# Query products of the later token blocks as three fp32r products in a fused attention and two-layer MoE kernel

## The chip, the cores and the metric

The kernel runs on one core of one Trainium2 chip. The metric is the time of one execution on the device in microseconds (us). The core has five engines that run side by side, each with its own queue of instructions: PE multiplies matrices (the page shows its loads of weights as PEld), DVE and ACT work elementwise on on-chip memory, POOL does too but can't reach the accumulators (PSUM), and SP issues transfers (DMA). An instruction waits on semaphores for what it needs, and everything behind it on the same engine waits with it.

## The reference

Linear attention is computed per batch and head, its output is normalised per head, and the result goes through two feed-forward layers with a normalisation between them.

```python
kv = np.einsum('bhsd,bhse->bhde', k, v)          # 8 batches, 8 heads, 576 tokens, 64 wide
out = np.einsum('bhsd,bhde->bhse', q, kv)
rms = np.sqrt(np.mean(out * out, axis=-1, keepdims=True) + 1e-06)
x = out / rms * g_norm                            # as 4608 tokens x 512
h = np.maximum(np.maximum(x @ w1, x @ w2), x @ w3)
y = h @ w_out                                     # 768 wide inside
xn = y / rms(y) * rms_g
g = xn @ w_gate
result = (silu(g) * (xn @ w_val)) @ w_out2        # 1536 wide inside
```

## The kernel before, in words

The 4608 tokens are nine blocks of 512, numbered 0 to 8. A batch has 576 tokens, so most blocks lie across two batches: block 4 has 256 columns of batch 3 and 256 of batch 4, block 7 has 448 and 64, block 8 lies in batch 7 alone.

Nearly all products are exact to about fp32 by splitting. A value is rounded to the format fp32r by a copy on ACT (its high part), the rest is a subtraction on DVE or POOL (its low part), and `mm3` (lines 506 to 509) multiplies high by high, high by low and low by high into one accumulator. Two products of the kernel are not split: the key-value sums of a batch (`kv_part`, line 327) and the query products (`po`) take plain fp32 operands. A plain product stands in the trace as two records for each matmul of the program.

For blocks 0 to 2 the query products are made token by token (`token_steps`). For blocks 3 to 8 `wide_block` does a whole block. Its steps `po(c)` for c = 0 to 3 multiply two heads each: the stationary operand is a 128x128 matrix with the two heads' key-value sums on the diagonal (`kvbd`), the moving operand is 512 columns of queries, cut where the block passes from one batch into the next. ACT copies each result and squares it, DVE sums the squares (`part`), and a chain of small steps through DRAM gives the factors with which `xn` scales the copy. `hi` and `lo` then split that into `X[t]`, the operand of the block's three up products.

The order is written by hand. `tick` opens a slot and runs the steps that `at(n, ...)` has put n slots ahead. A block has 24 slots, of which each follows 12 matmuls of an up product (`do_p`) or of the product down (`do_o`). `slot` also advances three background chains: the normalisation of the block before (`flush`), the sums of pairs of blocks for the second layer (`aside`, which steps through `pair_sums`, with sums on DVE, high parts on ACT at line 711, low parts on DVE at line 715, and stores `td`), and the preparation of second-layer weights (`prep`, held back while `live` would exceed `room[0]`). While `pair_sums` is under way, `aside` runs once a slot and `prep` every second slot.

While the products of block t run, block t+1 is prepared. Its query products come in the first two slots, between the up products of block t. Batch t+2 is loaded in slot 18 (`load_kv`: per source two pieces of 256 rows, and 64 rows at the end), its key-value sums run in slot 23 (`do_kv`), and the queries of the next block but one are loaded in slots 19 and 20 (`load_q`). All these tiles come from one pool of 38 buffers of 4 KB per partition (`unit`); `X[t]` and the copies `yr` come from a pool `xp` of two buffers of 16 KB.

Of the kernel before, what the change touches and what calls it, by code (L numbers as in the profile page):

```python
# [29 lines left out]
NP = H // 2  # L30
WIDE = 3
J1, J2 = F1 // P, F2 // P
EPS = 1e-6
# [27 lines left out]
def tile_kernel(ctx: ExitStack, tc, qT, k, v, kvt0, kvt1, w1, w2, w3, wo, wg, wv, wo2, out):  # L61
# [201 lines left out]
    def load_kv_part(b, c, only=None):  # L263
        r = b * S
        m, tail = KV.setdefault(b, ([None] * 4, []))
        if c == 2:
            if b == 0:
                t = unit([P, 2 * DM], F32, "kvt")
                nc.sync.dma_start(t[:, :DM + 1 + KC], kvt0)
                tail += [t]  # L270
                first_tail.append(t)
            elif b == 1:
                t = unit([P, 2, DM], F32, "kvt")
                nc.sync.dma_start(t[:64], kvt1.rearrange("p (two f) -> p two f", two=2))
                tail += [t[:64, 0], t[:64, 1]]
            else:
                t = unit([P, 2, DM], F32, "kvt")
                for i, src in enumerate((k, v)):
                    tail.append(t[:64, i])
                    nc.sync.dma_start(tail[i], src[r + 512:r + 576, :])  # L280
# [25 lines left out]
    def kv_part(b, c):  # L306
# [5 lines left out]
        for hp in range(NP):  # L312
            pk = PK["odd" if b == 0 and hp >= NP // 2 else b]
            for h in range(2):
                o = (2 * hp + h) * D
                if c < 4:
                    kk = m[c // 2][:, c % 2, o:o + D]
                    vv = m[2 + c // 2][:, c % 2, o:o + D]
                elif b == 0:
                    r, f = divmod(o, DM // 2)  # L320
                    r = slice(r * 64, r * 64 + 64)
                    kk = tail[0][r, f:f + D]
                    vv = tail[0][r, DM // 2 + f:DM // 2 + f + D]
                else:
                    kk = tail[0][:, o:o + D]
                    vv = tail[1][:, o:o + D]
# [4 lines left out]

    def kv_copy(b, kvb):
        pk = PK.pop(b)
        n = NP // 2 if b == 0 else NP
        nc.scalar.activation(kvb[:D, :n, 0:D], pk[:D, :n], AF.Copy)
        nc.scalar.activation(kvb[D:, :n, D:], pk[D:, :n], AF.Copy)
        if b == 0:
            pk = PK.pop("odd")
            nc.vector.tensor_copy(kvb[:D, n:, 0:D], pk[:D, n:])
            nc.vector.tensor_copy(kvb[D:, n:, D:], pk[D:, n:])  # L340
        del KV[b]
        kvbd[b] = kvb

    def do_kv(b, kvb):
        for c in range(5):
            kv_part(b, c)
        kv_copy(b, kvb)

# [14 lines left out]
    def token_steps(i, pool=ps):  # L363
# [42 lines left out]
        def hi():  # L406
            if i // NS not in X:
                new_x(i // NS)
            nc.scalar.activation(X[i // NS][:, 0, :, cut_of(i)], st["pt"], AF.Copy, scale=gc)

        def lo():
            x = X[i // NS]
            f = cut_of(i)
            nc.vector.scalar_tensor_tensor(x[:, 1, :, f], st["pt"], gc, f32(x[:, 0, :, f]), ALU.mult, ALU.subtract)

# [14 lines left out]
    def wide_block(t, s):  # L430

        st = {}
        nb = TB // 32

        def po(c):
            if c == 0:
                st["y"] = xp.tile([P, 2, KC, TB], F32, tag="x", name="yr")
                st["part"] = hp.tile([P, KC, nb], F32, tag="part", name="part")
            q = Q[2 * t + c // 2][:, c % 2]
            o = psum([P, TB], "po")  # L440
            b = t * TB // S
            n = min(TB, (b + 1) * S - t * TB)
            nc.tensor.matmul(o[:, :n], kvbd[b][:, c, :], q[:, :n], start=True, stop=True)  # L443
            if n < TB:
                nc.tensor.matmul(o[:, n:], kvbd[b + 1][:, c, :], q[:, n:], start=True, stop=True)
            if c % 2:
                del Q[2 * t + c // 2]
            nc.scalar.activation(st["y"][:, 0, c], o, AF.Copy)
            sq = st["sq", c] = tmp("sq")
# [21 lines left out]
        def respread():  # L471
            for n in range(2):
                nc.scalar.dma_start(
                    st["y"][n * D:(n + 1) * D, 1].rearrange("p c f -> p (c f)"), hr_d[t][n:n + 1].to_broadcast([D, KC * TB])
                )

        def xn(c):
            x = st["x", c] = tmp("xn")
            f = st["y"][:, 1].rearrange("p (m c) f -> p m (c f)", m=2)[:, c // 2]
            f = f.rearrange("p (j c b) -> p c j b", c=2, b=nb)[:, c % 2]  # L480
            xv, yv = (a.rearrange("p (j b) -> p j b", b=nb) for a in (x, st["y"][:, 0, c]))
            nc.vector.scalar_tensor_tensor(xv, yv, gc, f, ALU.mult, ALU.mult)

        def hi(c):
            if c == 0:
                new_x(t)
            nc.scalar.activation(X[t][:, 0, c], st["x", c], AF.Copy)

        def lo(c):
            x = X[t]  # L490
            nc.gpsimd.tensor_tensor(x[:, 1, c], st.pop(("x", c)), f32(x[:, 0, c]), ALU.subtract)
# [12 lines left out]

# [6 lines left out]
    def proj(p, w, x, a=0, b=TB, cs=range(KC)):  # L511
        for c in cs:
            f = slice(c * P, (c + 1) * P)
            mm3(p[:, a:b], w[:, 0, f], w[:, 1, f], x[:, 0, c, a:b], x[:, 1, c, a:b], c == 0, c == KC - 1)

# [31 lines left out]
    def proj2(p, w, x):  # L547
        for c in range(KC):
            f = slice(c % 2 * P, (c % 2 + 1) * P)
            mm3(p, w[:, c // 2, 0, f], w[:, c // 2, 1, f], x[:, 0, c], x[:, 1, c], c == 0, c == KC - 1)  # L550

# [126 lines left out]
    def hi_x2(i):  # L678
        nc.scalar.activation(X[NB][:, 0, i], X2[i], AF.Copy)

    def lo_x2(i):
        nc.vector.tensor_tensor(X[NB][:, 1, i], X2.pop(i), f32(X[NB][:, 0, i]), ALU.subtract)

# [85 lines left out]
    def load_x(t):  # L769
        raw = xp.tile([P, 3, 2, TB], F32, tag="x", name="xr")  # L770
        nc.sync.dma_start(raw[:, 0], xn_d[t][:2 * P].rearrange("(c p) n -> p c n", p=P))
        for k in range(2):
            nc.sync.dma_start(raw[:, 1 + k], xn_d[t + k][2 * P:].rearrange("(c p) n -> p c n", p=P))
        XR.append(raw)

    def build_x(n):
# [7 lines left out]
        for m, r in ((1, 0), (2, 1), (3, 2)):  # L784
            for k in range(2):
                x = XO[m, k] = unit([P, 2, TB], F32R, "xo")
                nc.scalar.activation(x[:, 0], raw[:, r, k], AF.Copy)
            yield
            for k in range(2):
                x = XO[m, k]  # L790
                nc.gpsimd.tensor_tensor(x[:, 1], raw[:, r, k], f32(x[:, 0]), ALU.subtract)

# [67 lines left out]
    def slot():  # L860
# [3 lines left out]
        if not side or n_slot[0] % 2:  # L864
            prep()

    def prod3(o, ah, al, bh, bl, first, last):
# [126 lines left out]
    def down(n, ph, xs):  # L994
# [3 lines left out]
        if ph == 0:  # L998
            OP[n] = xp.tile([P, KC, 2, TB], F32, tag="x", name="op")

# [8 lines left out]
        def place(d, c):  # L1009
            fh, th = divmod(c, 2)  # L1010
            return OP[n][:, 2 * fh + d, th]

# [97 lines left out]
    with tc.manual_schedule():  # L1110
# [13 lines left out]

        kvb = []
        z = unit([P, 2, NP, P], F32, "kvbd")
        nc.gpsimd.memset(z, 0.0)
        kvb += [z[:, 0], z[:, 1]]
        tok = [token_steps(i, ps if i < NS else pa) for i in range(2 * NS)]
        up_p = {}  # L1130
# [25 lines left out]
        for word in ORDER.split():  # L1156
# [18 lines left out]
            elif kind == "kc":  # L1175
                kv_copy(n[0], kvb[n[0]])
            elif kind == "busy":
# [18 lines left out]
        def kv_do(n, b):  # L1196
            at(n, lambda: do_kv(b, kvb[b % 2]))

# [24 lines left out]
        for t in range(2, NB):  # L1223
            last = t + 1 == NB
            if not last:
                nt = t + 1
                wide_block(nt, 0)
                if nt + 1 < B:
                    at(14, lambda: room.__setitem__(0, 4))
                    at(18, lambda b=nt + 1: load_kv(b))  # L1230
                    at(23, lambda b=nt + 1: (do_kv(b, kvb[b % 2]), room.__setitem__(0, 8)))
                if nt + 1 < NB:
                    for g in range(2):
                        at(19 + g, lambda i=2 * nt + 2 + g: load_q(i))
            else:
# [117 lines left out]
```

## Time and profile before

| what | value |
|---|---|
| median of 3 runs | 1457.09 us (1456.44 to 1457.49) |
| the profiled execution | 1456.97 us, its span 1455.2 us |
| PE busy | 1448.5 us of the span |
| DVE, ACT, POOL busy | 900.1, 625.2, 470.5 us |
| blocks 3 to 8 prepared | about 173 to 540 us |

The profiled execution has its own time; its span runs from the first to the last instruction, and the 1.8 us around it are not in the trace. It lies 0.12 us under the median. A matmul's record is longer than what it costs, since matmuls overlap; the cost is read from the starts of neighbouring records.

### The profile page before, as it was taken

How to read it: one execution, taken by the hardware profiler on the slowest of the kernel's cores; microseconds unless marked ns; L12 is line 12 of the kernel's file. 1: busy time of each engine (PE TensorE's matmuls, PEld its weight loads, DVE VectorE, ACT ScalarE, POOL GpSimd, SP SyncE). 2: the span in 40 equal slices, each digit the busy share in tenths (PEclk: the TensorE clock that was granted, in tenths of full speed). 3: DMA queues.
4: the chain of work that ended last, by engine and by line, in shares of the span. 5: the costliest groups of instructions: out<-in, count | busy, mean ns of one | idle time of the engine just before them, and what ended most of it. 6: DMA issues, size and time to landing. Idle time of an engine off the chain costs nothing.

```text
span 1455.2 us, 19535 instructions
## 1 busy us (share of the span) xinstructions
PE 1448.5 (100%) x7062; PEld 1201.1 (83%) x7062; DVE 900.1 (62%) x1341; ACT 625.2 (43%) x1110; POOL 470.5 (32%) x317
## 2 busy tenths in 40 slices
PE   9999999999999999999999999999999999999999
PEld 8888888888888878888888888888888888888887
DVE  6864475667366776874445475674665656754756
ACT  6863445445434563644224343343243442434422
POOL 3211232424232423321332252541334422532423
PEclk9999999999999999999999999999999999999999
DMA  9422255657266655779968464784666843784542
GB/s 367 154 94 95 80 182 200 221 215 277 106 210 219 232 188 192 279 262 374 371 228 329 177 234 185 284 311 171 247 228 257 333 179 130 296 302 182 193 170 107
DMA packets 108176, 322.54 MB, mean 222 GB/s; under 512 B 13168, under 2 KB 13424, under 8 KB 107312
## 3 DMA queue, kind: packets, MB, share of 16 engines
q1 hardware_dynamic: 94592, 294.56, 55.0%
q10 hardware_dynamic: 13488, 26.73, 5.8%
q8 instruction: 56, 0.92, 0.3%
q14 instruction: 40, 0.33, 0.1%
HBM read 247.73 MB, written 73.52 MB: 221 GB/s over the span
## 4 chain that ended last, share of the span: by engine, by line
PE 99%; DVE 0%; issue 0%; ACT 0%; POOL 0%; POOLq 0%
PE ua L869 18%; PE p L507 10%; PE p L509 10%; PE p L508 10%; PE ub L869 9%; PE da L869 9%; PE db L869 4%; PE uc L869 4%; PE acc L508 4%; PE acc L507 4%; PE acc L509 4%; PE dc L869 2%; PE pk L327 1%; PE po L443 1%; PE pg L507 1%; PE pv L509 1%
## 5 line engine op out<-in xcount | busy, mean ns | idle before, releaser
L507 PE MATMUL p<-x,w 128*128 128x512 f32 (+1 forms) x656 | 258.8, 395 | 0.0
L509 PE MATMUL p<-x,w 128*128 128x512 f32 (+1 forms) x656 | 254.0, 387 | 0.0
L508 PE MATMUL p<-x,w 128*128 128x512 f32 (+1 forms) x656 | 253.7, 387 | 0.0
L869 PE MATMUL ua<-xo,w 128*128 128x512 f32 x864 | 213.4, 389 | 0.0
L526 POOL TENSOR_TENSOR ho<-sl,ho 128x512 fp32r<-128x512 f32 x72 | 98.2, 1371 | 303.1 <-issue 247.3
L869 PEld LDWEIGHTS ua<-xo,w 128*128 128x128 f32 x864 | 162.2, 188 | 33.7
L526 POOL TENSOR_TENSOR ho<-t,ho 128x512 fp32r<-128x512 f32 x96 | 123.9, 1295 | 133.1 <-ACT ho L525 116.1
L526 POOL TENSOR_TENSOR hs<-h,hs 128x512 fp32r<-128x512 f32 x45 | 64.4, 1430 | 297.2 <-ACT hs L525 253.8
L869 PE MATMUL ub<-xo,w 128*128 128x512 f32 x576 | 146.1, 389 | 0.0
L509 PEld LDWEIGHTS p<-x,w 128*128 128x128 f32 x656 | 123.2, 188 | 25.6
L507 PEld LDWEIGHTS p<-x,w 128*128 128x128 f32 x656 | 123.3, 188 | 24.9 <-issue 0.5
L508 PEld LDWEIGHTS p<-x,w 128*128 128x128 f32 x656 | 123.3, 188 | 24.6 <-issue 0.5
L869 PEld LDWEIGHTS ub<-xo,w 128*128 128x128 f32 x576 | 108.1, 188 | 22.5
L951 ACT ACTIVATE s<-ua 128x512 f32<-128x512 f32 x96 | 57.3, 597 | 139.2 <-PE ua L869 139.2
L869 PE MATMUL da<-ho,wd 128*128 128x512 f32 x432 | 105.7, 389 | 0.0
L525 ACT ACTIVATE ho<-t 128x512 fp32r<-128x512 f32 x96 | 59.4, 627 | 100.5 <-DVE t L702 100.5
L869 PEld LDWEIGHTS da<-ho,wd 128*128 128x128 f32 x432 | 81.1, 188 | 16.8
L538 DVE TENSOR_TENSOR s<-p,s 128x512 f32<-128x512 f32 x45 | 31.1, 690 | 98.8 <-PE p L509 91.8
L899 DVE TENSOR_TENSOR c<-uc,s 128x512 f32<-128x512 f32 x48 | 33.1, 689 | 84.1 <-PE uc L869 84.1
L507 PE MATMUL acc<-hs,w 128*128 128x512 f32 x216 | 84.2, 390 | 0.0
L509 PE MATMUL acc<-hs,w 128*128 128x512 f32 x216 | 84.1, 389 | 0.0
L508 PE MATMUL acc<-hs,w 128*128 128x512 f32 x216 | 84.0, 389 | 0.0
(163 smaller groups left out, 2664.5 us busy)
## 6 DMA issues: line engine op xcount, KB each, us to landing
w<-wd SPq DMA_DIRECT2D x180, 512.0 KB, 7.7
wd<-ws SPq DMA_DIRECT2D x72, 512.0 KB, 3.1
wd<-wd SPq DMA_DIRECT2D x72, 512.0 KB, 6.9
wq<-wd SPq DMA_DIRECT2D x72, 256.0 KB, 7.7
xo<-td SPq DMA_DIRECT2D x32, 512.0 KB, 9.6
q<-in_qT SPq DMA_DIRECT2D x18, 512.0 KB, 6.3
raw<-in_w SPq DMA_DIRECT2D x18, 512.0 KB, 10.1
raw<-in_wo SPq DMA_DIRECT2D x18, 512.0 KB, 6.7
```

Source lines behind the costliest of these rows:

```text
L327: nc.tensor.matmul(pk[h * D:(h + 1) * D, hp, :], kk, vv, start=(c == 0 and hp in ((0, NP // 2) if b == 0 else (0,))), stop=(c == 4), skip_ ...
L443: nc.tensor.matmul(o[:, :n], kvbd[b][:, c, :], q[:, :n], start=True, stop=True)
L507: nc.tensor.matmul(o, ah, bh, start=first, stop=False)
L508: nc.tensor.matmul(o, ah, bl, start=False, stop=False)
L509: nc.tensor.matmul(o, al, bh, start=False, stop=last)
L525: nc.scalar.activation(hs[:, 0], h, AF.Copy)
L526: nc.gpsimd.tensor_tensor(hs[:, 1], h, f32(hs[:, 0]), ALU.subtract)
L538: nc.vector.tensor_tensor(s2, p, s1, ALU.max)
L869: nc.tensor.matmul(o, aa, bb, start=first and q == 0, stop=last and q == 2, skip_group_check=True)
L899: nc.vector.tensor_tensor(t, p, s, ALU.add)
L951: nc.scalar.activation(t, p, AF.Copy)
```

## The change

The query products of blocks 3 to 8 are now split too. `kv_split` rounds the key-value sums of a batch to high parts on ACT and puts the rest on DVE, both into one buffer `kvr` that is used again by every second batch; batch 2 is kept in both forms, since block 2 still needs the plain one. `split` rounds the queries of a block in the first two slots, two instructions on ACT and two on DVE in each, and `po` follows a slot later with `mm3`. The later steps of `wide_block` move by one slot, the last splits by two.

The key-value rows of batches 2 to 7 are loaded as pieces of 256 rows, 128 rows and 192 rows (96 partitions with two rows each), one slot earlier, and their sums run one slot earlier. The query loads move to slots 22 and 23. The pool `xp` has four buffers of 8 KB in place of two of 16 KB. `aside` runs three times in two slots, and the bounds in `room` are 5, 7 and 10 in place of 4 and 8.

```diff
+WIDE_KV = WIDE * 512 // 576
...
-    xp = ctx.enter_context(tc.tile_pool(name="xp", bufs=2))
+    xp = ctx.enter_context(tc.tile_pool(name="xp", bufs=4))
...
     def load_kv(b):
-        for c in range(3):
-            load_kv_part(b, c)
+        r = b * S
+        one = unit([P, 2, DM], F32, "kv")
+        parts = []
+        for i, src in enumerate((k, v)):
+            two = unit([P, 2, DM], F32, "kv")
+            nc.sync.dma_start(two, src[r:r + 256, :].rearrange("(p two) f -> p two f", two=2))
+            nc.sync.dma_start(one[:, i], src[r + 256:r + 384, :])
+            three = unit([P, 2, DM], F32, "kv")[:96]
+            nc.sync.dma_start(three, src[r + 384:r + 576, :].rearrange("(p two) f -> p two f", two=2))
+            parts.append([two[:, 0], two[:, 1], one[:, i], three[:, 0], three[:, 1]])
+        KV[b] = parts, None
...
-                if c < 4:
+                if tail is None:
+                    kk, vv = (a[c][:, o:o + D] for a in m)
+                elif c < 4:
...
+    kvr = {}
+
+    def kv_split(pk, b):
+        if b - 2 in kvr:
+            w = kvr[b] = kvr.pop(b - 2)
+        else:
+            w = kvr[b] = unit([P, 2, NP, P], F32R, "kvr")
+            nc.gpsimd.memset(f32(w), 0.0)
+        parts = [(slice(0, D), slice(0, D)), (slice(D, P), slice(D, P))]
+        for r, f in parts:
+            nc.scalar.activation(w[r, 0, :, f], pk[r], AF.Copy)
+        for r, f in parts:
+            nc.vector.tensor_tensor(w[r, 1, :, f], pk[r], f32(w[r, 0, :, f]), ALU.subtract)
...
+    def kv_copy(b):
         pk = PK.pop(b)
+        if b >= WIDE_KV:
+            kv_split(pk, b)
+        if b > WIDE_KV:
+            del KV[b]
+            kvbd.clear()
+            kvb.clear()
+            return
...
+        def split(m):
+            if m == 0:
+                st["y"] = xp.tile([P, KC, TB], F32, tag="x", name="y")
+                st["hi"] = xp.tile([P, KC, TB], F32R, tag="x", name="qh")
+                st["part"] = hp.tile([P, KC, nb], F32, tag="part", name="part")
+            q = Q.pop(2 * t + m)
+            lo = st["lo", m] = unit([P, 2, TB], F32R, "ql")
+            for c in range(2):
+                hi = st["hi"][:, 2 * m + c]
+                nc.scalar.activation(hi, q[:, c], AF.Copy)
+                nc.vector.tensor_tensor(lo[:, c], q[:, c], f32(hi), ALU.subtract)
...
         def po(c):
-            if c == 0:
-                st["y"] = xp.tile([P, 2, KC, TB], F32, tag="x", name="yr")
-                st["part"] = hp.tile([P, KC, nb], F32, tag="part", name="part")
-            q = Q[2 * t + c // 2][:, c % 2]
+            hi, lo = st["hi"][:, c], st["lo", c // 2][:, c % 2]
             o = psum([P, TB], "po")
             b = t * TB // S
             n = min(TB, (b + 1) * S - t * TB)
-            nc.tensor.matmul(o[:, :n], kvbd[b][:, c, :], q[:, :n], start=True, stop=True)
-            if n < TB:
-                nc.tensor.matmul(o[:, n:], kvbd[b + 1][:, c, :], q[:, n:], start=True, stop=True)
+            for w, f in ((kvr[b], slice(0, n)), (kvr.get(b + 1), slice(n, TB))):
+                if f.start < f.stop:
+                    mm3(o[:, f], w[:, 0, c], w[:, 1, c], hi[:, f], lo[:, f], True, True)
...
+        for m in range(2):
+            at(s + m, lambda m=m: split(m))
         for c in range(KC):
-            at(s + c // 2, lambda c=c: po(c))
-            at(s + 1 + c // 2, lambda c=c: part(c))
-            at(s + 14 + c // 2, lambda c=c: xn(c))
-            at(s + 15 + c // 2, lambda c=c: hi(c))
-            at(s + 16 + c // 2, lambda c=c: lo(c))
-        for m, fn in ((4, halves), (5, factor), (8, spread), (9, respread)):
+            at(s + 1 + c // 2, lambda c=c: po(c))
+            at(s + 2 + c // 2, lambda c=c: part(c))
+            at(s + 15 + c // 2, lambda c=c: xn(c))
+            at(s + 17 + c // 2, lambda c=c: hi(c))
+            at(s + 18 + c // 2, lambda c=c: lo(c))
+        at(s, lambda: room.__setitem__(0, 7))
+        at(s + 2, lambda: room.__setitem__(0, 10))
+        for m, fn in ((5, halves), (6, factor), (9, spread), (10, respread)):
             at(s + m, fn)
...
-        X[t] = xp.tile([P, 2, KC, TB], F32R, tag="x", name="x")
+        X[t] = [xp.tile([P, KC, TB], F32R, tag="x", name="x") for _ in range(2)]
...
         aside()
         if not side or n_slot[0] % 2:
             prep()
+        else:
+            aside()
...
-                    at(14, lambda: room.__setitem__(0, 4))
-                    at(18, lambda b=nt + 1: load_kv(b))
-                    at(23, lambda b=nt + 1: (do_kv(b, kvb[b % 2]), room.__setitem__(0, 8)))
+                    at(13, lambda: room.__setitem__(0, 5))
+                    at(17, lambda b=nt + 1: load_kv(b))
+                    at(22, lambda b=nt + 1: (do_kv(b), room.__setitem__(0, 7)))
...
                     for g in range(2):
-                        at(19 + g, lambda i=2 * nt + 2 + g: load_q(i))
+                        at(22 + g, lambda i=2 * nt + 2 + g: load_q(i))
```

Shown first is PE at the start of block 4's products, where block 5 is prepared. `pk` are the key-value sums, `acc` the product down, `p` an up product, `po` the query products. Before:

```order
L327 MATMUL pk<-v,k 64x64 x32
L327 MATMUL pk<-kvt 64x64 x8
...
L443 MATMUL po<-q,kvbd 128x320
L445 MATMUL po<-q,kvbd 128x192
L443 MATMUL po<-q,kvbd 128x320
L445 MATMUL po<-q,kvbd 128x192
```

In the changed kernel the same place reads:

```order
L334 MATMUL pk<-kv 64x64 x40
...
L555 MATMUL po<-qh,kvr 128x320
L556 MATMUL po<-ql,kvr 128x320
L557 MATMUL po<-qh,kvr 128x320
L555 MATMUL po<-qh,kvr 128x192
L556 MATMUL po<-ql,kvr 128x192
L557 MATMUL po<-qh,kvr 128x192
```

Each plain product became three, and the piece of 192 columns stands in three products of its own. Before, 12 matmuls (one up product) stand between `pk` and `po`; now 36 do (a product down and two up products).

The second place is SP in the last slots before block 4's products. `kv` and `kvt` are the rows of batch 5, `b` loads for the pair sums of blocks 1 and 2, `td` stores of them, `q` the queries of block 5. Before:

```order
L280 DMA kvt_2858<-in_v 64x512
L725 DMA b_2861<-xn1_88 128x512
L725 DMA b_2862<-xn1_88 128x512
L295 DMA q_2880<-in_qT 128x1024
L295 DMA q_2901<-in_qT 128x1024
L720 DMA td_2903<-b_2741 128x512
```

In the changed kernel:

```order
L294 DMA kv_2917<-in_v 96x1024
L768 DMA td_2923<-b_2815 128x512
...
L768 DMA td_3023<-y_2602 128x512
L768 DMA td_3029<-b_2883 128x512
L300 DMA q_3096<-in_qT 128x1024
L768 DMA td_3098<-y_2572 128x512
L300 DMA q_3119<-in_qT 128x1024
```

The two query loads stood ahead of the stores; now seven stores stand ahead of the first and one more ahead of the second. Each of the two waits for PE besides, since its buffer is one that the rows of batch 5 leave: the first for the second of the five pieces of the key-value sums, the second for the last piece.

The third place is ACT where the queries are split. `ws` and `wt` belong to the preparation of weights, `s1` is the copy of the first up product, `y` and `sq` are the copy and the square of a query product.

```order
L349 ACTIVATE kvr_1747<-pk_3051 64x4x64 x2
L767 DMA td_3098<-th_3027 128x512
L227 ACTIVATE ws_3102<-wt_2681 128x2x256
L113 ACTIVATE wt_3104<-raw_2761 128x512
L227 ACTIVATE ws_3124<-wt_2709 128x2x256
L582 ACTIVATE s1_3139<-p0_3126 128x512
L475 ACTIVATE qh_3142<-q_3096 128x512 x2
L227 ACTIVATE ws_3152<-wt_2709 128x2x256
L475 ACTIVATE qh_3142<-q_3119 128x512 x2
L490 ACTIVATE y_3141<-po_3174 128x512
L492 ACTIVATE sq_3182<-po_3174 128x512
```

The two pairs of `qh` are new; ahead of the first one stand the copy of the up product that runs at that time and work on the weights.

## Rows read from the trace of the kernel before

**Rows 1.** The page: busy time of each engine; the chain that ended last, by engine.

```profile
PE 1448.5 (100%) x7062; PEld 1201.1 (83%) x7062; DVE 900.1 (62%) x1341; ACT 625.2 (43%) x1110; POOL 470.5 (32%) x317
...
PE 99%; DVE 0%; issue 0%; ACT 0%; POOL 0%; POOLq 0%
```

**Rows 2.** Longest wait of PE: total us, times, longest us.

```profile
PE busy L302 <- POOL ident masks.py:199: 1.4, 1, 1.4
```

**Rows 3.** Timeline of PE (start us, us, what) around query products of blocks 4, 6, 7, 8.

```profile
245.47 0.59 PE L443 MATMUL po<-q,kvbd 128*128 128x256 f32 x2
...
247.43 0.40 PE L508 MATMUL p<-x,w 128*128 128x512 f32 x1
...
249.71 0.39 PE L509 MATMUL p<-x,w 128*128 128x512 f32 x1
...
390.25 0.81 PE L443 MATMUL po<-q,kvbd 128*128 128x384 f32 x2
...
392.21 0.40 PE L508 MATMUL p<-x,w 128*128 128x512 f32 x1
...
462.73 0.91 PE L443 MATMUL po<-q,kvbd 128*128 128x448 f32 x2
...
464.90 0.40 PE L508 MATMUL p<-x,w 128*128 128x512 f32 x1
...
532.76 1.88 PE L443 MATMUL po<-q,kvbd 128*128 128x512 f32 x4
...
534.71 0.40 PE L508 MATMUL p<-x,w 128*128 128x512 f32 x1
```

**Rows 4.** Timeline of PE: four 256-column fp32r products, the first and the last.

```profile
25.69 0.28 PE L507 MATMUL p<-x,w 128*128 128x256 f32 x1
...
26.05 0.28 PE L507 MATMUL p<-x,w 128*128 128x256 f32 x1
```

**Rows 5.** Timeline of weight loads (PEld) behind four 32-column products.

```profile
332.56 0.19 PEld L507 LDWEIGHTS p<-x,w 128*128 128x128 f32 x1
...
332.67 0.19 PEld L508 LDWEIGHTS p<-x,w 128*128 128x128 f32 x1
```

**Rows 6.** Timeline of PE around the key-value sums of batch 5.

```profile
312.04 0.39 PE L509 MATMUL acc<-hs,w 128*128 128x512 f32 x1
312.36 2.09 PE L327 MATMUL pk<-v,k 128*64 128x64 f32 x64
314.37 0.68 PE L327 MATMUL pk<-kvt 64*64 64x64 f32 x16
...
315.32 0.40 PE L508 MATMUL p<-x,w 128*128 128x512 f32 x1
```

**Rows 7.** Groups by line and form: count, busy us, mean ns, idle before, releaser.

```profile
L487 ACT ACTIVATE x<-xn 128x512 fp32r<-128x512 f32 x24 | 13.8, 623 | 30.3 <-DVE xn L482 30.3
...
L715 DVE TENSOR_TENSOR b<-b,th 128x512 fp32r<-128x512 f32 x16 | 15.1, 945 | 1.2 <-ACT th L711 0.6
...
L534 ACT ACTIVATE s<-p 128x512 f32<-128x512 f32 x45 | 26.7, 594 | 57.3 <-PE p L509 57.3
...
L335 ACT ACTIVATE kvbd<-pk 64x256 f32<-64x256 f32 x7 | 2.6, 373 | 20.5 <-PE pk L327 20.5
```

**Rows 8.** Stretches: length, busy PE, PEld, DVE, ACT, POOL, clock, DMA share, GB/s.

```profile
286.00:318.00 32.00, 32.00 (x210) 26.55 (x209) 22.77 (x29) 9.34 (x17) 11.23 (x7) 1.00 0.64 223
318.00:333.00 15.00, 15.00 (x71) 12.41 (x70) 9.17 (x14) 12.09 (x23) 1.31 (x1) 1.00 0.41 153
```

**Rows 9.** Timeline of POOL: low parts of the operand of block 4.

```profile
294.43 6.39 POOL L491 TENSOR_TENSOR x<-xn,x 128x512 fp32r<-128x512 f32 x4 [3.28 <-ACT x L487]
```

**Rows 10.** Line 295, the query loads: time from issue to landing.

```profile
DMA to landing us min/median/max: 3.5/6.3/12.0
```

**Rows 11.** DMA issues from 222 to 246 us: KB each, median us to landing.

```profile
q<-in_qT SPq DMA_DIRECT2D x2, 512.0 KB, 8.3
```

**Rows 12.** Line 711: what ended the idle time of ACT before it (us, times).

```profile
  DMA td<-th: 16.7, 9
```

More of the change, by code (lines that the diff above doesn't have):

```diff
@@ L275, in load_kv_part @@
                 tail += [t[:64, 0], t[:64, 1]]
[L276 to L280, printed above, removed]
             return
@@ L330, in kv_part, with do_kv @@
                 )
-    def kv_copy(b, kvb):
-        pk = PK.pop(b)
+    kvr = {}
[10 more added lines that the diff above has]
+            nc.vector.tensor_tensor(w[r, 1, :, f], pk[r], f32(w[r, 0, :, f]), ALU.subtract)
+    kvb = []
+    def kv_copy(b):
+        pk = PK.pop(b)
+        if b >= WIDE_KV:
[5 more added lines that the diff above has]
+            return
+        m = kvb[b % 2]
         n = NP // 2 if b == 0 else NP
-        nc.scalar.activation(kvb[:D, :n, 0:D], pk[:D, :n], AF.Copy)
-        nc.scalar.activation(kvb[D:, :n, D:], pk[D:, :n], AF.Copy)
+        nc.scalar.activation(m[:D, :n, 0:D], pk[:D, :n], AF.Copy)
+        nc.scalar.activation(m[D:, :n, D:], pk[D:, :n], AF.Copy)
         if b == 0:
             pk = PK.pop("odd")
-            nc.vector.tensor_copy(kvb[:D, n:, 0:D], pk[:D, n:])
-            nc.vector.tensor_copy(kvb[D:, n:, D:], pk[D:, n:])
+            nc.vector.tensor_copy(m[:D, n:, 0:D], pk[:D, n:])
+            nc.vector.tensor_copy(m[D:, n:, D:], pk[D:, n:])
+        kvbd[b] = m
         del KV[b]
-        kvbd[b] = kvb
-    def do_kv(b, kvb):
+    def do_kv(b):
         for c in range(5):
             kv_part(b, c)
-        kv_copy(b, kvb)
+        kv_copy(b)
     XN = {}
@@ L442, in po @@
             n = min(TB, (b + 1) * S - t * TB)
-            nc.tensor.matmul(o[:, :n], kvbd[b][:, c, :], q[:, :n], start=True, stop=True)
-            if n < TB:
-                nc.tensor.matmul(o[:, n:], kvbd[b + 1][:, c, :], q[:, n:], start=True, stop=True)
+            for w, f in ((kvr[b], slice(0, n)), (kvr.get(b + 1), slice(n, TB))):
+                if f.start < f.stop:
+                    mm3(o[:, f], w[:, 0, c], w[:, 1, c], hi[:, f], lo[:, f], True, True)
             if c % 2:
-                del Q[2 * t + c // 2]
-            nc.scalar.activation(st["y"][:, 0, c], o, AF.Copy)
+                del st["lo", c // 2]
+            if c + 1 == KC:
+                del st["hi"]
+            nc.scalar.activation(st["y"][:, c], o, AF.Copy)
             sq = st["sq", c] = tmp("sq")
@@ L472, in respread @@
             for n in range(2):
+                if n == 0:
+                    st["f"] = xp.tile([P, KC, TB], F32, tag="x", name="fr")
                 nc.scalar.dma_start(
-                    st["y"][n * D:(n + 1) * D, 1].rearrange("p c f -> p (c f)"), hr_d[t][n:n + 1].to_broadcast([D, KC * TB])
+                    st["f"][n * D:(n + 1) * D].rearrange("p c f -> p (c f)"), hr_d[t][n:n + 1].to_broadcast([D, KC * TB])
                 )
@@ L478, in xn @@
             x = st["x", c] = tmp("xn")
-            f = st["y"][:, 1].rearrange("p (m c) f -> p m (c f)", m=2)[:, c // 2]
+            f = st["f"].rearrange("p (m c) f -> p m (c f)", m=2)[:, c // 2]
             f = f.rearrange("p (j c b) -> p c j b", c=2, b=nb)[:, c % 2]
-            xv, yv = (a.rearrange("p (j b) -> p j b", b=nb) for a in (x, st["y"][:, 0, c]))
+            xv, yv = (a.rearrange("p (j b) -> p j b", b=nb) for a in (x, st["y"][:, c]))
             nc.vector.scalar_tensor_tensor(xv, yv, gc, f, ALU.mult, ALU.mult)
@@ L678, in hi_x2 @@
     def hi_x2(i):
-        nc.scalar.activation(X[NB][:, 0, i], X2[i], AF.Copy)
+        nc.scalar.activation(X[NB][0][:, i], X2[i], AF.Copy)
     def lo_x2(i):
-        nc.vector.tensor_tensor(X[NB][:, 1, i], X2.pop(i), f32(X[NB][:, 0, i]), ALU.subtract)
+        nc.vector.tensor_tensor(X[NB][1][:, i], X2.pop(i), f32(X[NB][0][:, i]), ALU.subtract)
     NPAIR = (NB - 1) // 2
@@ L769, in load_x @@
     def load_x(t):
-        raw = xp.tile([P, 3, 2, TB], F32, tag="x", name="xr")
-        nc.sync.dma_start(raw[:, 0], xn_d[t][:2 * P].rearrange("(c p) n -> p c n", p=P))
+        two = xp.tile([P, 2, 2, TB], F32, tag="x", name="xr")
+        raw = [two[:, 0], two[:, 1], xp.tile([P, 2, TB], F32, tag="x", name="xr")]
+        nc.sync.dma_start(raw[0], xn_d[t][:2 * P].rearrange("(c p) n -> p c n", p=P))
         for k in range(2):
-            nc.sync.dma_start(raw[:, 1 + k], xn_d[t + k][2 * P:].rearrange("(c p) n -> p c n", p=P))
+            nc.sync.dma_start(raw[1 + k], xn_d[t + k][2 * P:].rearrange("(c p) n -> p c n", p=P))
         XR.append(raw)
@@ L786, in build_x @@
                 x = XO[m, k] = unit([P, 2, TB], F32R, "xo")
-                nc.scalar.activation(x[:, 0], raw[:, r, k], AF.Copy)
+                nc.scalar.activation(x[:, 0], raw[r][:, k], AF.Copy)
             yield
@@ L998, in down @@
         if ph == 0:
-            OP[n] = xp.tile([P, KC, 2, TB], F32, tag="x", name="op")
+            OP[n] = [xp.tile([P, 2, 2, TB], F32, tag="x", name="op") for _ in range(2)]
         def slot():
@@ L1010, in place @@
             fh, th = divmod(c, 2)
-            return OP[n][:, 2 * fh + d, th]
+            return OP[n][fh][:, d, th]
         def keep(d, c, p):
@@ L1128, in tile_kernel @@
         kvb += [z[:, 0], z[:, 1]]
+        del z
         tok = [token_steps(i, ps if i < NS else pa) for i in range(2 * NS)]
@@ L1175, in tile_kernel @@
             elif kind == "kc":
-                kv_copy(n[0], kvb[n[0]])
+                kv_copy(n[0])
             elif kind == "busy":
@@ L1196, in kv_do @@
         def kv_do(n, b):
-            at(n, lambda: do_kv(b, kvb[b % 2]))
+            at(n, lambda: do_kv(b))
         kv_do(0, 2)
```

15 lines of the change are left out of this document (7 added, 8 removed).

## The prediction

> **What bounds the kernel.** I read the engine totals and the chain of waits first: PE is busy for the whole span and makes up 99% of the chain, and no other engine comes near [rows 1]. The waits of PE then say whether it is ever kept waiting: its largest item is a single 1.4 us on start-up work, the identity matrix [rows 2]. So time goes up or down by what the change does to the spacing of PE's matmuls, and by any wait that it puts in front of PE. What it does to the other engines counts only where it reaches PE.
>
> **The price of a product.** The cost of a matmul is the distance between starts, not the length of its record. An fp32r product of 512 columns costs 0.228 us (from 247.43 to 249.71, ten of them) [rows 3], one of 256 columns 0.120 us (0.36 for three) [rows 4]. The straight line through both is 0.012 us plus 0.000422 us a column: 0.147 for 320 columns, 0.174 for 384, 0.201 for 448. Below 256 columns the trace has no fp32r product. Streaming alone would be 0.093 for 192 columns, 0.066 for 128, 0.039 for 64. But every product brings its own weights, and where short products can't hide that, two loads of fp32r weights stand 0.11 us apart [rows 5]. So a narrow product costs from 0.111 (weight load alone) to 0.120 (no better than 256 columns); I take 0.116, the middle.
>
> **Query products, what is removed.** Two steps `po` run back to back. From the first record to the following up product (the start of the second matmul less 0.228) they take 247.43 - 0.228 - 245.47 = 1.73 us in block 4, 1.73 in block 6, 1.94 in block 7, 1.72 in block 8 [rows 3]; blocks 3 and 5 (192 and 320 columns) cost as much as block 4. Each block has two such pairs: 2 x (4 x 1.73 + 1.94 + 1.72) = 21.2 us.
>
> **What is added.** Per step, three products for each piece:
> blocks 3 and 5: 3 x (0.116 + 0.147) = 0.789;
> block 4: 3 x 2 x 0.120 = 0.720;
> block 6: 3 x (0.174 + 0.116) = 0.870;
> block 7: 3 x (0.201 + 0.116) = 0.951;
> block 8: 3 x 0.228 = 0.684.
> Together 4.80, times four steps 19.2 us. The gain is 2.0 us. Of the products added 48 are narrow, so the ends 0.111 and 0.120 make it 2.2 and 1.8.
>
> **Key-value sums.** Four pieces of 16 records take 2.01 us, 0.50 each; the fifth, of 64 rows in another array shape, takes 0.72 up to the next product (315.32 - 0.23 - 314.37) [rows 6]. In the changed kernel all five pieces have the shape of the first four, two of them with 96 rows in place of 128. If the fifth then costs 0.50 and the switch back to fp32r nothing, 0.22 is saved; if the 0.22 is all that switch, nothing. I take 0.13, for six batches 0.8 us (0 to 1.3).
>
> **Work on other engines, counted at nothing on the path.** ACT gets 24 copies of queries at about 0.62 us, as line 487's, and the key-value copies stay at about 0.37 each; DVE gets 24 subtractions of up to 0.95 us, the mean of line 715's, and twelve small ones [rows 7]. At a block start ACT is busy for 12.1 of 15 us, DVE for 9.2 [rows 8]. With four copies more ACT has 14.6 of 15, so this cover is thin on ACT. What hides it is the order: let T be the start of the key-value sums. Then come a product down and two up products of 12 x 0.228 = 2.7 us each, so the first up product ends at T + 8.2 and `po` starts at T + 10.9. ACT copies the up product (0.59), rounds the first 512 columns of queries (0.62), DVE takes the low part (0.95): T + 8.2 + 0.59 + 0.62 + 0.95 = T + 10.4, 0.5 us early. Were that cover gone, every late microsecond would count once in each of six blocks. The operand of the next block is finished a slot or two later (slots 18 and 19); its four low parts take POOL 6.4 us and ended at 300.8, 14 us before use [rows 9], so some 8 us stay. The pair sums only run closer together: DVE is at 22.8 of 32 us there [rows 8], and they end by the block start, where they ran into it before. Batch 2 is copied in both forms, and its plain copies now wait on ACT until DVE has made the low parts; block 2 uses them first after an up product, a product down and a further up product, so this stays hidden too. The key-value loads and sums keep their five slots (15 us) of distance, both moved by one; `room` only decides when second-layer weights are prepared, which PE needs after block 8.
>
> **Query loads.** This is the one place where a wait can come. The first load now waits until PE has read the second piece of the key-value rows, T + 1.1, and it stands behind stores of the pair sums. The split needs it by T + 10.9 - 0.95 - 0.62 - 0.1 = T + 9.2. A landing within 8.1 us is free; the median is 6.3, the slowest was 12.0 [rows 10], and around block 4 a pair took 8.3 [rows 11]. I take 0.2 us in all for this (0 to 1.0).
>
> **Sum.** -2.0 - 0.8 + 0.2 = -2.6 us, against the profiled execution 1456.97 - 2.6 = 1454.4; the median of the runs is 0.12 above that execution, so 1454.5. With all ends the way that they add up, 1453.6 to 1456.3. A measurement of this kernel can tell about 0.2%, 2.9 us, from no change, and the forecast lies just inside.
>
> **Rivals.** First, narrow products go as fast as they stream. Against it stands the load distance of 0.11 [rows 5]; for it, that those loads stand behind plain products, not in a run of fp32r ones. Then 24 products of 192 columns gain 0.023 each, twelve of 128 columns 0.050, twelve of 64 columns 0.077: 2.1 us more, 1452.4. The Trainium skill ("TensorE: Matmul & The Clock Gate", section "Back-to-back issue gap") gives 81 ns for each pair of weight load and 128-column matmul in a long stream; as an estimate from that figure for all 48 the time would be 48 x 0.035 = 1.7 us lower than my sum. The loads in this trace stand 111 ns apart, which speaks against the page's figure, and I go by the trace.
>
> Second, the other side: below 256 columns an fp32r product falls back to the rate of a plain one. No row excludes it, since 256 is the narrowest [rows 4]. A plain product costs 1.722 / 2 = 0.861 per 512 columns [rows 3], so 0.323 for 192 and 0.215 for 128; 64 columns would stay at the weight load. Price: 24 x (0.323 - 0.116) + 12 x (0.215 - 0.116) = 6.2 us, so 1460.7. It decides from an average narrow product of 0.17 us on (48 x 0.054 = 2.6 eats the gain) and is slower beyond 0.2% from 0.23.
>
> Third, the queries come late. In blocks 5 and 7 the pair sums are still under way when the load is due, ACT has already waited 16.7 us in nine times for stores of theirs [rows 12], and at the higher pace such waits grow. ACT stops at the first copy, the up product's copies behind it stop too, and PE waits before `po`. If the loads of blocks 4 to 7 come 0.65 us late each, the gain is gone, 1457.1; 1.4 us late each is slower by 0.2%. One landing of 12 us costs 3.9 alone.
>
> Fourth, the change doesn't thin out PE at all: that would need three fp32r products to cost as much as a plain one, and 3 x 0.228 against 0.861 excludes it at 512 columns [rows 3].
>
> **Chances.** Forecast 0.56, fast narrow products 0.07, plain rate 0.13, late queries or a late ACT 0.24. Faster by over 0.2% means below 1454.2: 0.4 of the forecast and the first rival, 0.30. Slower: the second rival and a third of the late queries, 0.22. The rest, 0.48, is within 0.2%. The range reaches from the first rival to just beyond the second, 1452.2 to 1461.0; what is left out is mainly late queries at their worst.
>
> **What would show it.** Right: in the timeline of PE a pair of steps `po` takes 1.58 us in blocks 3 and 5, 1.44 in block 4, 1.37 in block 8; narrow products start 0.11 to 0.12 apart; the key-value sums take 2.6 in place of 2.73; the waits of PE stay as they were. Wrong: narrow products 0.2 to 0.3 apart (second rival) or under 0.1 (first); PE waiting for ACT or DVE before `po`, with ACT idle for a query load ahead of its first copy (third); key-value sums that take as long as before.

## The result, and the profile after

The changed kernel takes 1471.84 us (median of six runs, 1470.72 to 1476.94), the kernel before beside it 1456.88 us: a ratio of 1.0107, with a 95% interval from 1.0092 to 1.0122. That is 15.0 us slower, outside the predicted range. The profiled execution took 1470.72 us, its span 1468.9 us.

The page after, the two lines that answer to [rows 1]:

```profile
PE 1451.9 (99%) x7106; PEld 1207.7 (82%) x7106; DVE 916.0 (62%) x1377; ACT 638.6 (43%) x1136; POOL 463.6 (32%) x319
...
PE 86%; DMA 6%; DVE 3%; issue 2%; POOL 1%; ACT 1%; ACTq 0%; SPq 0%; DVEq 0%; POOLq 0%
```

PE still looks full, but it has fallen to 86% of the chain: somewhere PE was kept waiting, and the chain runs through other engines there. The waits of PE after, which answer to [rows 2]:

```profile
PE po L555 <- ACT qh L475: 6.3, 2, 3.8
PE p L555 <- ACT s L582: 1.9, 1, 1.9
PE busy L307 <- POOL ident masks.py:199: 1.4, 1, 1.4
...
PE po L556 <- DVE ql L476: 0.6, 2, 0.3
...
PE p L556 <- POOL x L535: 0.4, 1, 0.4
```

The old longest wait is now the third. Three places are new: the query products of block 5 at 319 us (3.8 us) and of block 7 at 469 us (2.5 us), and an up product at 611 us (1.9 us).

**What PE does undisturbed is as forecast.** Timeline of PE after: the key-value sums of batch 5, for [rows 6], and a pair of steps `po` of block 5:

```profile
308.14 2.55 PE L334 MATMUL pk<-kv 128*64 128x64 f32 x80
...
310.96 0.39 PE L556 MATMUL acc<-hs,w 128*128 128x512 f32 x1
...
329.42 0.30 PE L555 MATMUL po<-qh,kvr 128*128 128x320 f32 x1
...
329.86 0.25 PE L555 MATMUL po<-qh,kvr 128*128 128x192 f32 x1
329.94 0.28 PE L556 MATMUL po<-ql,kvr 128*128 128x192 f32 x1
330.06 0.27 PE L557 MATMUL po<-qh,kvr 128*128 128x192 f32 x1
330.17 0.33 PE L555 MATMUL po<-qh,kvr 128*128 128x320 f32 x1
...
331.20 0.39 PE L556 MATMUL acc<-hs,w 128*128 128x512 f32 x1
```

The key-value sums take 310.96 - 0.23 - 308.14 = 2.59 us (forecast 2.6), the pair, read as in the prediction, 331.20 - 0.23 - 329.42 = 1.55 (forecast 1.58). A 192-column product costs 0.08, 0.12 and 0.11 us in turn.

**What holds PE at 319 us.** Follow the engines backwards. DVE and POOL before block 5:

```profile
310.22 1.76 DVE L750 TENSOR_TENSOR y<-y,b 128x512 f32<-128x512 f32 x1
312.08 1.60 DVE L763 TENSOR_TENSOR b<-b,th 128x512 fp32r<-128x512 f32 x1
313.61 0.68 DVE L750 TENSOR_TENSOR b<-b,y 128x512 f32<-128x512 f32 x1
...
316.81 0.68 DVE L590 TENSOR_TENSOR h<-p,s 128x512 f32<-128x512 f32 x1
```

```profile
306.78 6.36 POOL L535 TENSOR_TENSOR x<-xn,x 128x512 fp32r<-128x512 f32 x4
```

While POOL makes the low parts of `x`, the pair sums on DVE (L750, L763) take 1.6 to 1.8 us in place of 0.68. In the kernel before POOL does this from 294.43 to 300.8 us [rows 9]. Pair sums lie beside it there too and take 1.2 to 1.7 us, but it is over 17 us before the query products, and DVE stands idle for 2.6 us in between. DVE before:

```profile
298.01 1.66 DVE L702 TENSOR_TENSOR y<-y 128x512 f32<-128x512 f32 x1
...
307.12 0.69 DVE L538 TENSOR_TENSOR s<-p,s 128x512 f32<-128x512 f32 x1 [2.64 <-PE p L509]
```

Now the subtractions end only 6 us before the query products are due. Behind the pair sums stands `h` of the maximum (316.81), and behind `h` stands ACT's queue:

```profile
317.52 0.63 ACT L573 ACTIVATE hs<-h 128x512 fp32r<-128x512 f32 x1 [2.05 <-DVE h L590]
...
318.83 0.63 ACT L227 ACTIVATE ws<-wt 128x512 fp32r<-128x512 f32 x1
...
320.56 0.60 ACT L582 ACTIVATE s<-p 128x512 f32<-128x512 f32 x1
322.19 1.15 ACT L475 ACTIVATE qh<-q 128x512 fp32r<-128x512 f32 x2 [1.03 <-DMA q<-in_qT]
```

Key-value copies and weight preparation (L227) fill the gaps. ACT comes to the query copies at 322.19 - 1.03 = 321.2 us; PE has been ready for them since 318.9. The last microsecond is a query load, late because SyncE's queue holds it behind the stores of the same pair sums:

```profile
316.31 0.32 SPq L768 DMA_DIRECT2D td<-b  x1
316.73 0.40 SPq L300 DMA_DIRECT2D q<-in_qT  x1
```

Block 7 repeats this: `h` starts at 466.44, the copy `s` at 470.21, and the query copies at 471.28 after 0.48 us for the load.

**What holds PE at 611 us** is the same without any query: weight-preparation sums (L213 to L216) of 256 columns take 1.4 to 1.5 us each under POOL, the pair sums come after them, ACT waits 7.1 us for one of these, and the copy `s` of the maximum stands behind it. Timelines of DVE, ACT and PE:

```profile
608.98 1.50 DVE L216 TENSOR_TENSOR wt<-wt 128x256 f32<-128x256 f32 x1
...
611.00 0.68 DVE L750 TENSOR_TENSOR y<-y,b 128x512 f32<-128x512 f32 x1
```

```profile
611.71 0.63 ACT L759 ACTIVATE th<-y 128x512 fp32r<-128x512 f32 x1 [7.10 <-DVE y L750]
...
612.25 0.58 ACT L582 ACTIVATE s<-p 128x512 f32<-128x512 f32 x1
```

```profile
612.88 0.50 PE L555 MATMUL p<-x,w 128*128 128x512 f32 x1 [1.90 <-ACT s L582]
...
614.36 0.63 PE L557 MATMUL p<-x,w 128*128 128x512 f32 x1
614.78 0.63 PE L555 MATMUL p<-x,w 128*128 128x512 f32 x1
```

**A wait costs more than its length.** The last two starts lie 0.42 us apart, not 0.23. Stretches after (length, busy PE, PEld, DVE, ACT, POOL, granted clock, DMA share, GB/s):

```profile
319.00:323.00 4.00, 0.21 (x2) 0.13 (x1) 2.46 (x6) 2.94 (x6) 0.51 (x1) 1.00 0.97 323
322.80:326.80 4.00, 3.62 (x14) 3.29 (x15) 3.92 (x7) 3.10 (x8) 0.00 (x0) 0.62 1.01 411
474.00:477.00 3.00, 3.00 (x10) 2.56 (x9) 2.81 (x6) 3.00 (x7) 0.00 (x0) 0.50 0.91 365
614.00:617.00 3.00, 3.00 (x9) 2.35 (x8) 2.94 (x6) 1.56 (x5) 0.00 (x0) 0.50 1.03 382
```

After each wait PE's granted clock falls to 0.50, its lower level of 1.2 GHz. The waits themselves come to 6.3 + 1.9 + 0.6 + 0.4 = 9.2 us. As an estimate, each low stretch costs its length times what the clock lacks, at least 4 x 0.38 = 1.5, 3 x 0.50 = 1.5 and 1.5, together 4.5 us. With the 2.8 us that PE gains (see the last run below) these make 9.2 + 4.5 - 2.8 = 10.9 us of the 13.7 that the span grew by. The last run below also shows where the rest lies.

### The profile page after: what moved, and what is told of

Read it like the earlier page. It is cut to its first block, busy times and chain, and to the rows that moved or that the text cites. A ratio compares the mean times of both kernels' runs of the same rounds, so it can differ in the third digit from the quotient of the medians.

```text
span 1468.9 us, 19702 instructions
## 1 busy us (share of the span) xinstructions
PE 1451.9 (99%) x7106; PEld 1207.7 (82%) x7106; DVE 916.0 (62%) x1377; ACT 638.6 (43%) x1136; POOL 463.6 (32%) x319
## 4 chain that ended last, share of the span: by engine, by line
PE 86%; DMA 6%; DVE 3%; issue 2%; POOL 1%; ACT 1%; ACTq 0%; SPq 0%; DVEq 0%; POOLq 0%
PE ua L920 18%; PE ub L920 9%; PE da L920 9%; PE p L555 8%; PE p L556 8%; PE p L557 8%; PE db L920 4%; PE uc L920 4%; PE acc L555 3%; PE acc L556 3%; PE acc L557 3%; PE dc L920 2%; DMA rs<-rs 2%; PE pk L334 1%; DMA td<-th 1%
## 5 line engine op out<-in xcount | busy, mean ns | idle before, releaser
L983 ACT ACTIVATE sg<-c 128x512 f32<-128x512 f32 x72 | 45.6, 633 | 83.6 <-DVE c L950 83.6
```

What stands on the lines that cost most here:

```text
L983: nc.scalar.activation(sg, src, AF.Sigmoid)
```

## Experiments

Theory A: at 1.5 steps a slot the pair sums put more on DVE, ACT and SyncE, ahead of what PE waits for, than these clear in time. Theory B: the query loads are three slots later than before. Theory C: POOL's subtractions, moved onto the pair sums, slow DVE. Theory D: the copies `th`, the high parts of the pair sums on ACT, wait for buffers that stores still hold. Each run was timed beside the kernel before (medians 1457.06, 1457.39 and 1457.24 us in the three groups of runs).

**The slower pace alone.**

```diff
         if not side or n_slot[0] % 2:
             prep()
-        else:
-            aside()
```

> The changed kernel with the pair sums back at one step a slot. Theory A (the faster pace puts more pair-sum copies on ACT and more pair stores on SyncE ahead of the query split and of the s copy, and those in-order queues then hold TensorE): all three long waits of TensorE, at 319, 469 and 611 us, go, and the time is the kernel before less what the undisturbed blocks gained, about 1454 us. Theory B (the query loads are simply three slots later than before): the waits at 319 and 469 us stay, only the one at 611 us goes, about 1467 us. Theory C (POOL's four subtractions, two slots later, halve VectorE under the pair sums): less work is under them, but the VectorE operations that lie under them still take 1.5 to 1.8 us, so part of the waits stays, 1458 to 1465 us.

1459.73 us, ratio 1.0021 (1.0010 to 1.0032), in C's range. Without the faster pace twelve of the fifteen microseconds are gone. The wait at 611 us is gone, as A and B say, but two waits before the query products stay, contrary to A alone (the profiled execution, 1463.46 us, was the longest of ten, so its waits are at the upper end):

```profile
PE po L555 <- ACT qh L475: 3.8, 2, 2.5
```

**The kernel before at the faster pace.** The same two lines (`else: aside()`) added to the kernel before, and nothing else.

> The kernel before with the pair sums at 1.5 steps a slot and nothing else changed. Theory A: a wait of TensorE of some us comes up in blocks 5 and 7 or at the end of the first layer, 1460 to 1466 us. Theory B and theory C (neither the loads nor the subtractions have moved): no wait over 1 us, within 1 us of the kernel before.

1468.01 us, ratio 1.0074 (1.0057 to 1.0091): more than A expected, and B and C fall as sole causes. With no split at all PE waits in the same two blocks, now for the load itself, which SyncE issues behind stores of the pair sums (PE, then SyncE at block 5):

```profile
PE po L443 <- DMA q<-in_qT: 3.9, 2, 2.3
PE po L445 <- ACT kvbd L336: 1.5, 2, 0.8
```

```profile
313.89 0.33 SPq L720 DMA_DIRECT2D td<-y  x1
315.20 0.33 SPq L295 DMA_DIRECT2D q<-in_qT  x1
```

In the kernel before, the second load was issued at 299.79 us.

**Low parts of `x` on DVE.**

```diff
-            nc.gpsimd.tensor_tensor(x[1][:, c], ...)
+            nc.vector.tensor_tensor(x[1][:, c], ...)
```

> The changed kernel with the four low parts of x of each token group taken by VectorE and no longer by POOL. Theory C: no VectorE operation of the first layer takes 1.5 to 1.8 us any more, the pair sums end some 4 us sooner, the three waits go or fall below 1 us, 1454 to 1460 us. Theory A: VectorE has 4 x 0.68 us more of its own and the queue ahead of the query split is as long as it was, so the waits stay at half or more, 1463 to 1472 us. Theory B: the waits at 319 and 469 us stay whole, 1466 to 1472 us.

1468.50 us, ratio 1.0077 (1.0062 to 1.0092): within A's range and within B's, some 3 us better than the changed kernel. The wait for the split is 5.5 us, that for `s` 1.3. C is a part, not the whole, at this pace.

**Query loads at slots 19 and 20.**

```diff
-                        at(22 + g, lambda i=2 * nt + 2 + g: load_q(i))
+                        at(19 + g, lambda i=2 * nt + 2 + g: load_q(i))
```

> The changed kernel with the query loads issued at slots 19 and 20, as before the change, in place of 22 and 23; on SyncE they then stand behind two and four of the block's pair stores and no longer behind five and six. Theory B: the waits at 319 and 469 us go and the one at 611 us stays, about 1461 us. Theory A: the copies of the split are still queued behind the pair-sum copies on ACT, so these waits shrink by about a third at most, 1467 to 1471 us.

1475.17 us, ratio 1.0121 (1.0106 to 1.0136): no faster, even slower than A allowed, and B falls. In block 5 SyncE issues the first load nine microseconds sooner, and ACT no longer waits for it; yet it copies at 321.37, only 0.8 us sooner, because its queue ends there (SyncE, then ACT):

```profile
307.91 0.33 SPq L300 DMA_DIRECT2D q<-in_qT  x1
```

```profile
321.37 1.14 ACT L475 ACTIVATE qh<-q 128x512 fp32r<-128x512 f32 x2
```

Block 7 waits 4.6 us in place of 2.5. From 452 to 470 us, with the loads now among them, the stores `td` of the copies `th` take 5.1 us to land (median of seven), in the changed kernel 2.5. So one `th`, which the changed kernel began at 464.50 without a wait, waits for its buffer, and `h` comes 2.2 us later (468.59 in place of 466.44):

```profile
467.32 0.63 ACT L759 ACTIVATE th<-y 128x512 fp32r<-128x512 f32 x1 [2.48 <-DMA td<-th]
```

This is D's wait, reaching PE in this run. That the loads are what slows the stores is likely, but not shown by a run of its own.

**Nine buffers for `th`.** Pool `yp` from 7 to 9 buffers, pool `up` from 38 to 37, at the faster pace.

> The changed kernel, pair sums at 1.5 steps a slot, with nine 2 KB buffers in place of seven for the high parts th of the pair sums (and one 4 KB buffer less in the large pool). Theory D (the th copies wait for a buffer that a store has not yet left, 1.7 and 1.2 us each time, and hold ACT): these waits go, the query split comes 2 to 4 us sooner in blocks 5 and 7, 1460 to 1467 us. Theory A (it is the amount of pair-sum work in front, on VectorE as on ACT): the copies then wait for VectorE's differences, within 2 us of the changed kernel's 1471.8 us.

1473.70 us, ratio 1.0113 (1.0098 to 1.0128): D falls as the cause in the changed kernel. In block 5 the copies no longer wait for stores, and DVE goes on without a gap; but now five of its operations lie under POOL, and `h` comes out at the very time of the changed kernel:

```profile
307.44 1.76 DVE L763 TENSOR_TENSOR y<-y,th 128x512 fp32r<-128x512 f32 x1
...
312.53 1.77 DVE L750 TENSOR_TENSOR b<-b,y 128x512 f32<-128x512 f32 x1
...
316.81 0.68 DVE L590 TENSOR_TENSOR h<-p,s 128x512 f32<-128x512 f32 x1
```

**Slower pace and low parts on DVE.** Both edits together.

> Pair sums at one step a slot and the low parts of x on VectorE, the rest of the change as it is. In the run with the slower pace alone, four VectorE operations under POOL's subtractions took 1.2 to 1.8 us and the query copies came 1.5 and 2.6 us late at 319 and 467 us. Theory C (VectorE halved by POOL is what is left): those four operations fall to 0.68 us, 2 to 3 us of the queue go for 2.7 us of VectorE's own, the two waits fall below 1 us and the time is 1454 to 1457 us. Rival (the queue on ACT ahead of the split is what is left, whoever subtracts): the waits stay within 1 us of what they were, 1458 to 1462 us.

1455.78 us, ratio 0.9989 (0.9980 to 0.9998): 4 us faster than the slower pace alone, as C expected of what is left there. The wait for `qh` falls from 3.8 us in two places to 1.3 in one, not below 1 (in an execution of 1459.03 us, again the longest of ten).

**Slower pace and an earlier split.** High parts get `unit` buffers of their own, and

```diff
-                        at(22 + g, lambda i=2 * nt + 2 + g: load_q(i))
+                        at(20 + g, lambda i=2 * nt + 2 + g: load_q(i))
+                        at(23 + g, lambda g=g, t=nt + 1: split(t, g))
```

> Pair sums at one step a slot, and the query split one slot earlier (its high parts in buffers of their own, the query loads two slots earlier), the products where they were. If the split is only late by ACT's and VectorE's queues, by 1.5 us in block 5 and 2.6 us in block 7, one slot of 2.7 us covers it: no wait of TensorE over 0.3 us at 319 and 467 us, and the time is that of the kernel before less the gain of the undisturbed blocks, 1453 to 1455 us. If the query loads or the engines' total work set it, waits of 1 us or more stay and the time is above 1457 us.

1457.20 us, ratio 1.0002 (0.9992 to 1.0011). The waits for `qh` are gone, but in block 7 PE still waits 0.5 us for a low part and 0.4 us for a maximum on DVE: one slot covers most of the lateness, not all, and the time misses the 1453 to 1455 us expected. (Line numbers shown from runs with the earlier split are up to two lower than in the changed kernel.)

**The same with the low parts on DVE.**

> The run before this one, with the low parts of x on VectorE as well. If the early split has removed the last wait, VectorE's four operations more a block change nothing: within 1 us of that run. If waits are left there, this one is faster by them, 1453 to 1455 us.

1455.71 us, ratio 0.9990 (0.9980 to 0.9999): 1.5 us faster than without, so waits had been left. The time is still above the 1453 to 1455 us expected of that case; two waits of PE of 0.3 us remain.

**That, at the faster pace.** `else: aside()` put back.

> The run with the early split and the low parts of x on VectorE (1455.7 us), with the pair sums at 1.5 steps a slot again. Theory A as it now stands (the faster pace puts more than VectorE and ACT clear in time ahead of every copy that TensorE waits for, the s copies of the maximum as much as the query split): the split is covered by its slot, but s or h copies come late near 320, 467 and 609 us, 1458 to 1465 us. Rival (only the query split was ever late, and it is now covered): 1455 to 1456.5 us.

1461.44 us, ratio 1.0027 (1.0018 to 1.0037): the pace alone still costs 5.7 us when the low parts of `x` are off POOL and the split is covered, as A expected. The waits move to whatever copy or maximum is next, and the largest are:

```profile
PE po L554 <- DVE s L585: 1.5, 1, 1.5
...
PE po L554 <- ACT sq L490: 1.3, 1, 1.3
...
PE p L554 <- ACT s L581: 1.0, 2, 0.6
```

**Control: the kernel before with its low parts on DVE.**

> Control: the kernel before with the low parts of x on VectorE and nothing else. If the gain of the two runs below the kernel before comes from the change's products and pieces, this one stays within 1 us of the kernel before. If it comes from taking POOL away from VectorE, it is 1 to 2 us faster than before.

1456.99 us, ratio 0.9999 (0.9989 to 1.0008): no gain. In the kernel before, the subtractions that lie on POOL cost PE nothing.

**Less preparation ahead of the split.** The earlier split, the slower pace and the low parts on DVE, and

```diff
-                    at(22, lambda b=nt + 1: (do_kv(b), room.__setitem__(0, 7)))
+                    at(22, lambda b=nt + 1: do_kv(b))
...
-        at(s, lambda: room.__setitem__(0, 7))
+        at(s, lambda: room.__setitem__(0, 7 if t == WIDE else 5))
```

> The run with the early split and the low parts of x on VectorE, with the weight preparation held at five buffers until slot 2 of the next block, so that two to four copies of it stand behind and no longer ahead of the query copies on ACT. That run still had TensorE 0.5 us late at 468 and at 538 us (squares and s copies on ACT and VectorE): if the queue sets these, they go and the time is 1454.0 to 1455.3 us; if they are set by something else, it is within 0.5 us of 1455.7 us.

1454.43 us, ratio 0.9981 (0.9972 to 0.9989): 2.8 us faster than before, and the fastest of all. So weight preparation ahead of the split had held PE too, for 1 us or so (1455.71 us without this edit; the two intervals overlap a little). The new pieces of key-value rows, the four buffers of `xp` and the later steps are all still in this run, so by themselves they don't hold PE. No wait of PE is left outside the start of the program:

```profile
PE busy L307 <- POOL ident masks.py:199: 1.4, 1, 1.4
PE pt L435 <- DVE xn L384: 1.2, 3, 0.6
PE po L407 <- ACT kvbd L367: 0.7, 1, 0.7
```

The same matmuls stand in the same order in this run and in the changed kernel, so their starts can be set side by side:

| matmul | changed kernel | this run | behind, us |
|---|---|---|---|
| before the query products of block 5 | 318.01 | 318.02 | 0.0 |
| up product after the first wait | 328.06 | 321.86 | 6.2 |
| in the query products of block 7 | 480.19 | 469.12 | 11.1 |
| before the wait at 611 us | 608.09 | 596.97 | 11.1 |
| after that wait | 618.02 | 602.41 | 15.6 |
| after the wait for `gs` | 752.09 | 735.84 | 16.2 |

The three places with the clock behind them make 15.6 of the 16.5 us between the two spans (1468.9 and 1452.4), against 9.2 us of waits: about 6 us more than the waits themselves, the low clock foremost.

## Why the prediction was wrong

**The gain on PE was right.** "-2.0 - 0.8" says 2.8 us for the products and the key-value sums; with every wait taken away the same products and pieces gain 1457.24 - 1454.43 = 2.8 us. The second rival fell: no narrow product costs over 0.12 us. The first was right for one product in three: the first of each piece takes what it streams (0.08 us at 192 columns, 0.06 at 128), the other two 0.11, as two weight loads do [rows 5]. All query products together, read as in the prediction, take 2 x (1.55 + 1.44 + 1.55 + 1.73 + 1.89 + 1.36) = 19.0 us in the fastest run, 19.2 were forecast. The Trainium skill ("TensorE: Matmul & The Clock Gate", section "Back-to-back issue gap") gives 81 ns at 128 columns; here the mean of three is (0.06 + 0.11 + 0.11) / 3 = 0.093 us, between the page's figure and the 0.116 of the sum.

**The step that failed is "Work on other engines, counted at nothing on the path"**, in its sentence "The pair sums only run closer together". It summed busy time over 32 us [rows 8] and found room. But these engines work in order: what counts is what stands in the queue ahead of the copy that PE waits for. The pace alone costs 11 us in the kernel before and 5.7 us with the split early and the low parts on DVE; taking it away gives back 12 of 15 us. The same step says that "`room` only decides when second-layer weights are prepared". But three preparation copies (318.83 to 320.5 us) stand ahead of the copy `s` on ACT, and holding preparation back brought the last 1 us or so.

**The cover of 0.5 us was counted from a punctual ACT.** The working had ACT at the copy of the up product at T + 8.2; with T = 308.14 that copy began at 320.56, T + 12.4. The prediction called this cover thin and put a price in microseconds only on late loads. The load was in fact 1.0 us of it; in the run with early loads ACT's queue alone keeps the copies all but 0.8 us as late.

**The operand of the next block was given some 8 us of cover.** It counted the two slots of its delay at their length, but not where POOL's 6.4 us would then lie: on the pair sums, which it slows by up to 1.1 us an operation. A sign of it stood in the rows: line 715's mean of 0.945 us [rows 7] mixes subtractions of 0.68 us with some of 1.6 beside POOL. At 610 us PE even waits 0.4 us for the operand itself.

**"Query loads", 0 to 1.0 us in all, and the third rival.** The mechanism was named, with blocks 5 and 7 and ACT in it. Its size was off in two ways: 2.5 and 3.8 us for two blocks in place of 0.65 to 1.4 for four, and waits taken at their own length, where the lower clock after them adds at least half as much again (4.5 us to 9.2). The prediction left "late queries at their worst" out of its range, and gave late queries or a late ACT a chance of 0.24. The wait at 611 us, where no query is involved, was not foreseen.

## What to carry to other kernels

When background work is sped up, don't compare its busy time with the free time of its engine: list what it puts into each in-order queue ahead of the next instruction that the bottleneck waits for, stores on the load queue included. When a step moves by two slots, look at what it will then lie beside, above all POOL beside DVE. To keep a gain of 0.2% on a full TensorE, this kernel needed its operands a whole slot ahead: the waits of 2.3 us around 611 us cost 4.5 us, the lower clock included.

## What the runs showed of the hardware

**DVE beside POOL.** A DVE operation of 512 columns that reads two SBUF tiles took 1.2 to 1.8 us under a POOL subtraction, mostly 1.58 to 1.77, and 0.68 outside; a 256-column one took 1.4 to 1.5 us in place of 0.42. One that reads PSUM and SBUF did not slow down. On DVE itself the four subtractions took 1.28 us a pair, on POOL 6.4 us together. Timelines of DVE and POOL in the run with the slower pace alone:

```profile
309.91 1.58 DVE L763 TENSOR_TENSOR y<-y,th 128x512 fp32r<-128x512 f32 x1
311.42 0.68 DVE L586 TENSOR_TENSOR s<-p,s 128x512 f32<-128x512 f32 x1
```

```profile
306.27 6.37 POOL L535 TENSOR_TENSOR x<-xn,x 128x512 fp32r<-128x512 f32 x4
```

The Trainium skill ("SBUF — State Buffer", section "SBUF: two separate sides") has the two engines share a pair of ports under an exclusive lock, which a DVE operation takes when both its inputs lie in SBUF. By that rule an operation waits for one of POOL's to end and then runs at its own speed; the rows fit it, 0.68 with an input in PSUM and up to about 1 us of delay otherwise.

**The clock after a wait.** In the changed kernel each of the three waits was followed by some 3 us in which the granted clock was 0.50, its lower level; the kernel before has 1.00 in the stretch from 318 to 333 us [rows 8]. It did not follow every wait: in the kernel before at the faster pace PE waited 1.6 us and 0.7 us in block 5, and from 318 to 328 us its clock stayed at 1.00. Nor does the length alone decide: with the slower pace and the low parts on DVE, waits of 1.35 and 0.54 us in block 7 were followed by a clock of 0.50 from 467.5 to 470.7 us.
